# Holding back one unit's loads at the start of a retention and mixer kernel, and moving three small steps of its first stage

## The chip, the cores and the metric

The kernel runs on one core of a Trainium2 chip. The metric is the device time of one execution in microseconds. Five runs of the kernel before gave 327.78 to 331.32 us, median 329.55 us.

The core has a matrix engine (PE, with its weight loads shown apart as PEld), a vector engine (DVE), a scalar engine (ACT), a general engine (POOL, GpSimd) and a synchronising engine (SP). Each works through its own instructions in order. In this kernel SP issues the loads of q, k and v and the DMA transposes; GpSimd issues the loads of the two weights and most stores. All transfers share the core's 16 DMA engines.

## What is computed

Two layers, one behind the other. The first is causal retention with a decay per head, over 8 batches, 8 heads, 576 positions and 64 features:

```python
scores = scale * np.matmul(q, k.transpose(0, 1, 3, 2))
gamma = 1.0 - 2.0 ** (-5.0 - np.arange(H, dtype=np.float32))
rel = pos[:, None] - pos[None, :]
Dmat = np.where(rel >= 0, gamma[:, None, None] ** rel[None, :, :], 0.0)
x = np.matmul(scores * Dmat, v)      # then heads side by side: (8, 576, 512)
```

The second mixes positions through a rank of 32 and then channels through a hidden layer of 2048:

```python
h = x.transpose(0, 2, 1) @ U @ V
u = x + h.transpose(0, 2, 1)
out = u + np.maximum(u @ w_ch1, 0.0) @ w_ch2
```

The decay from position j to position i is a product of a power of gamma at i and one at -j. So the kernel scales keys or values by `vscale` (gamma to the power -j, with the softmax-like scale in it) and outputs by `qscale` (gamma to the power i), and needs only a 0/1 triangle between them.

## The kernel before

Batches go in pairs. A pair has 2 x 576 = 1152 positions, nine chunks of 128; chunk 4 (J) is half of one batch and half of the other. `LO` is its lower half of the partitions (the end of the first batch), `HI` its upper half.

The steady part (from `first_stretch`'s end on) handles a chunk so: `load` brings q, k, v (SP), `cast_chunk` casts them to bf16 on ACT and DVE and scales the values on POOL, `xbar` transposes q and k with a DMA (L289, SP), and `section` does scores, state and outputs on PE. `merge` interleaves these steps with the two large matmuls of the mixer, `y1` (L525) and `y2` (L559), by fixed costs; the order on each engine is then the order of the program.

The first pair is different. Its eight whole chunks are taken as four units of 256 positions, numbered 0 to 3: units 0 and 1 are the first batch, 2 and 3 the second. Positions of a unit lie two to a partition. `load_u` (L615) loads a unit in six tiles, two halves of heads for each of k, q and v. `scale_u` (L643) scales the keys by the decay on POOL, `cast_u` (L636) casts q and v, `T_u` (L652) transposes with PE, `SC_u` and `mask_u` make scores, `RV_u` multiplies them with v, `ST_u` (L766) adds keys times values into a state in PSUM, `Sblk` (L776) copies the state to SBUF, `QS_u` multiplies queries with it, and `XS_u` multiplies the result by `qscale` and writes x. The functions with `_J` do the same for one half of chunk J.

`startup` (L867) writes the order by hand. It first puts all loads on SP: units 0 and 1, chunk J, unit 2, unit 3. On POOL it puts the casts of each unit in turn with pieces of the weight loads between them (`load_w1`, L194; for unit 2 the pieces 4 to 6, 6 to 8 and 8 to 10, for unit 3 the pieces 10 to 12 and 12 to 16), and all of the second weight's loads behind. PE computes the first batch's x, mixes it and gives the transposed result `uT`. `first_stretch` (L990) then works through units 2 and 3 on PE with blocks f = 0 to 15 of `y1` between their steps (`y(n)`: the next n blocks). Blocks 2 and 3 come between unit 2's transposes and its scores, block 4 behind those scores, 5 and 6 behind that; unit 3's transposes follow, then blocks 7 to 12 among unit 3's steps. Block f needs its piece of the first weight. `first_stretch` also puts the loads of the first four chunks of the second pair on SP, behind unit 3's loads.

Of the kernel before, what the change touches and what calls it, by code (L numbers as in the profile page):

```python
# [12 lines left out]
ALU = mybir.AluOpType  # L13
# [21 lines left out]
def kernel(  # L35
# [193 lines left out]
                    in_=dram[b, :, t0:t0 + n, :].rearrange("h s d -> s h d"),  # L229
                )  # L230

    def cast_qk(pr, i, rows=slice(0, P), eng_k=nc.vector, eng_q=nc.scalar):
        c = ch[pr, i]
        if "qk" not in c:
            c["qk"] = qk_pool.tile([P, 2, dm], BF16, tag="qk", name="qk")
        t = c["qk"]
        for j, e in ((1, eng_k), (0, eng_q)):
            o, f = t[rows, j, :], c["f", j][rows].rearrange("p h d -> p (h d)")
            if e is nc.scalar:
                nc.scalar.activation(out=o, in_=f, func=AF.Copy)  # L240
            else:
                e.tensor_copy(out=o, in_=f)
# [369 lines left out]
    def unit_i0(u):  # L612
        return 2 * u + (1 if u >= 2 else 0)

    def load_u(u, which):  # L615
        b = u // 2
        t0 = 2 * P * (u % 2) + HALF * b
        for j in which:
            dram = (q, k, v)[j]
            for hh in range(2):  # L620
                t = stage.tile([P, H, D], FP32, tag="stage", name="stage_t")
                un[u]["f", j, hh] = t
                nc.sync.dma_start(  # L623
                    out=t.rearrange("p (h j) d -> p h (j d)", j=2),
                    in_=dram[b, 4 * hh:4 * hh + 4, t0:t0 + 2 * P, :].rearrange(
                        "h (p j) d -> p h (j d)", j=2),
                )
# [53 lines left out]
    def SC_u(u, hh, pool_, tag):  # L681
        psc = pool_.tile([P, 2, NHP, P], FP32, tag=tag, name="psc")
        kT, qt = un[u]["T", 1], qT(u)
        for hp in range(2):
            for jj in range(2):
                for s in range(2):
                    for hl in range(2):
                        r = slice(hl * HALF, (hl + 1) * HALF)
                        m = slice(s * HALF, (s + 1) * HALF)
                        nc.tensor.matmul(  # L690
                            psc[m, hl, hp * 2 + jj, :], kT[r, jj * NHP + 2 * hh + hp, m],
                            qt[r, 2 * hh + hp, s * P:(s + 1) * P], start=True, stop=True,
                        )
        un[u]["psc", hh] = psc

    def mask_u(u, hh):
        ret = ret_pool.tile([P, H, P], BF16, tag="ret", name="ret")
        nc.vector.tensor_tensor(  # L698
            out=ret.rearrange("p (a j) i -> p a (j i)", j=2),
            in0=un[u]["psc", hh].rearrange("p a b i -> p (a b i)").rearrange(  # L700
                "p (a ji) -> p a ji", a=4),
            in1=triU.rearrange("p j i -> p (j i)")[:, None, :].to_broadcast([P, 4, 2 * P]),
            op=ALU.mult,
        )
        un[u]["ret", hh] = ret
# [60 lines left out]
    def ST_u(u, rows, acc, start, hps=range(4)):  # L766
        for hp in hps:
            for jj in range(2):
                nc.tensor.matmul(
                    acc[:, hp, :], un[u][1][rows, jj, hp * P:(hp + 1) * P],  # L770
                    un[u][2][rows, jj, hp * P:(hp + 1) * P],
                    start=(start and hp == 0 and jj == 0), stop=True,
                    skip_group_check=True,
                )

    def Sblk(acc, slot):  # L776
        for hl in range(2):
            r = slice(hl * HALF, (hl + 1) * HALF)
            nc.scalar.activation(
                out=sblk[r, slot, :, hl * D:(hl + 1) * D],  # L780
                in_=acc[r, :, hl * D:(hl + 1) * D], func=AF.Copy)
# [57 lines left out]

    def XS_J(r):  # L840
        c = ch[0, J]
        nc.vector.tensor_tensor(
            out=st["x", 0][r, J, :].rearrange("p (h d) -> p h d", d=D),
            in0=c["po"][r, :].rearrange("p (h d) -> p h d", d=D),
            in1=qscale[r, J, :, None].to_broadcast([HALF, H, D]), op=ALU.mult,
        )
# [19 lines left out]

    def startup():  # L867
        load_u(0, (1, 0))
        load_v_rows()
        load_u(1, (1, 0))  # L870
        load_u(0, (2,))
        load(0, J, (1, 0), seg=0)
        load_u(1, (2,))
        load(0, J, (2,), seg=0)
        load_u_rows()
        load(0, J, (1, 0, 2), seg=1)
        load_u(2, (1, 0, 2))
        load_u(3, (1, 0, 2))
        nc.gpsimd.memset(st["x", 0][HI, J, :], 0.0)

        warm(10)
        cast_unit(0)
        T_u(0, 1, nc.vector)
        un[0]["off"] = y1_tile(0)[:, 0:4, :].rearrange(
            "p (a x) (y i) -> p a (x y) i", x=2, i=P)
        nc.vector.memset(un[0]["off"][HI], 0.0)
        warm(5)
        nc.scalar.activation(out=V_b, in_=V_f, func=AF.Copy)
        T_u(0, 0, nc.scalar)
        make_v()  # L890
        warm(5)
        SC_u(0, 0, ps_sc, "psc")
        mask_u(0, 0)
        cast_unit(1)
        cast_u(0, 2, 0, nc.gpsimd)
        cast_u(0, 2, 1, nc.gpsimd)
        cast_u(1, 2, 0, nc.gpsimd)
        load_w1(0, 2)
        cast_u(1, 2, 1, nc.gpsimd)
        T_u(1, 1, nc.scalar)  # L900
        SC_u(0, 1, ps_o, "po")
        mask_u(0, 1)
        SC_off(0, ps_sc, "psc")
        warm(3)
        T_u(1, 0)
        SC_off(1, ps_o, "po")
        warm(3)
        SC_u(1, 0, ps_sc, "psc")
        mask_u(1, 0)
        SC_u(1, 1, ps_o, "po")  # L910
        mask_u(1, 1)
        cast_qk(0, J, LO, nc.scalar, nc.scalar)

        acc1 = pss_tile()
        ST_u(0, ALL, acc1, True)
        Sblk(acc1, 1)
        RV_u(0, 0)
        RV_u(0, 1)
        RV_off()
        XS_u(0)  # L920
        T_J(LO)
        acc2 = ps_big.tile([P, NHP, P], FP32, tag="big", name="pss2")
        ST_u(0, ALL, acc2, True)
        prep_v(0, J, LO)
        cast_urows()
        RV_u(1, 0)
        SC_J(LO)
        mask_J(LO)
        for hp in (0, 2):
            ST_u(1, LO, acc1, False, (hp, hp + 1))  # L930
            if hp == 2:
                Sblk(acc1, 2)
            ST_u(1, ALL, acc2, False, (hp, hp + 1))
        Sblk(acc2, 3)
        cast_qk(0, J, HI, nc.gpsimd, nc.gpsimd)
        prep_v(0, J, HI)
        load_w1(2, 4)
        for u in (2, 3):
            for hh in range(2):
                scale_u(u, hh, nc.gpsimd)  # L940
            load_w1(4 if u == 2 else 10, 6 if u == 2 else 12)
            for hh in range(2):
                cast_u(u, 0, hh, nc.gpsimd)
            load_w1(6 if u == 2 else 12, 8 if u == 2 else 16)
            cast_u(u, 2, 0, nc.gpsimd)
            cast_u(u, 2, 1, nc.gpsimd)
            if u == 2:
                load_w1(8, 10)
        for f in range(0, NF, 2):
            load_w2(f)  # L950
        RV_u(1, 1)
        QS_u(1, 0, 1)
        XS_u(1, 0, 1)
        RV_J(LO)
        QS_u(1, 1, 2)
        XS_u(1, 1, 2)
        QS_J(3)
        XS_J(LO)

        xT = [ps_big.tile([P, dm], FP32, tag="big", name="xT") for _ in range(3)]  # L960
        xT.append(ps_sc.tile([P, dm], FP32, tag="psc", name="xT"))

        def to_xT(lo, hi):
            for i in range(lo, hi):
                for cc in range(NCC):
                    nc.tensor.matmul(
                        xT[cc][:, i * P:(i + 1) * P],
                        st["x", 0][:, i, cc * P:(cc + 1) * P], ident,
                        start=(i == 0), stop=True, skip_group_check=True,
                    )  # L970

        to_xT(0, 2)
        MA, _, _, _ = mixer_items(0, 0, split=True)
        MA((ps_o, "po"))
        to_xT(2, J)
        for cc in range(NCC):
            g = slice(cc * R, (cc + 1) * R)
            nc.tensor.matmul(
                xT[cc], st["a", 0][g, :], V4[g, HALF:HALF + 4 * P],
                start=False, stop=True, skip_group_check=True,  # L980
            )
        for cc in range(NCC):
            o = st["uT", 0][:, :, cc, :]
            i_ = xT[cc].rearrange("p (s t) -> p s t", t=P)
            if cc % 2 == 0:
                nc.scalar.activation(out=o, in_=i_, func=AF.Copy)
            else:
                nc.vector.tensor_copy(out=o, in_=i_)
# [129 lines left out]
```

## Time and profile before

| what | us |
|---|---|
| median of five runs | 329.55 |
| the profiled execution | 330.45 |
| its span | 328.7 |
| PE busy | 313.4 |
| DVE busy | 170.3 |
| ACT busy | 143.9 |
| POOL busy | 102.1 |
| PE idle for weight loads (L525) before 80 us | 3.4 |
| unit 3's first load issued by SP | 24.62 |
| its scores' transposes done on PE | 43.24 |
| first chunk of the second pair used by PE | 71.54 |

The span is the time between the first and the last instruction that the profiler recorded; the execution's own time has 1.75 us more around it. A busy time is a sum over an engine's instructions. What a stage is limited by is read from the waits in it: the idle time before an instruction, and what released it.

### The profile page before, as it was taken

The numbers are of one execution on the slowest core, as the hardware profiler recorded it, in microseconds if no ns is written. First come the engines' busy times: TensorE is split into PE (matmuls) and PEld (weight loads), VectorE is DVE, ScalarE is ACT, GpSimd is POOL, SyncE is SP. The second block draws the span as 40 slices with busy tenths as digits, with TensorE's granted clock in tenths as the row PEclk, the third lists the DMA queues.
The fourth block names the chain that finished last, engine by engine and source line by source line (L and its number), as shares of the span: only waits on it lengthen the run. The fifth ranks groups of instructions, "written<-read, shape, count | busy, mean of one in ns | idle before, by whom it ended". The sixth has DMA issues, their size and how long they took to land.

```text
span 328.7 us, 9095 instructions
## 1 busy us (share of the span) xinstructions
PE 313.4 (95%) x3860; PEld 171.6 (52%) x3885; DVE 170.3 (52%) x332; ACT 143.9 (44%) x326; POOL 102.1 (31%) x170
## 2 busy tenths in 40 slices
PE   7998799999999999999999999999999999999996
PEld 3574454665444445456754444456744444467544
DVE  7663256625844477546764377546744475510022
ACT  2837355886002186028820385048810473037400
POOL 7579560342111733223421324142321500110000
PEclk9999799999999999999999999999999999999999
DMA  8999999896992989998999599868997460340012
GB/s 215 231 198 254 224 207 201 189 178 117 205 243 86 242 194 173 211 204 154 201 183 209 130 158 224 206 152 155 208 205 166 124 52 16 92 119 0 2 72 88
DMA packets 152904, 53.30 MB, mean 162 GB/s; under 512 B 132032, under 2 KB 150336, under 8 KB 152864
## 3 DMA queue, kind: packets, MB, share of 16 engines
q1 hardware_dynamic: 144512, 40.40, 66.3%
q0 software_dynamic: 8352, 12.32, 16.0%
q8 instruction: 30, 0.49, 0.7%
q14 instruction: 10, 0.08, 0.1%
HBM read 36.85 MB, written 9.44 MB: 141 GB/s over the span
## 4 chain that ended last, share of the span: by engine, by line
PE 77%; DMA 7%; SPq 5%; ACT 4%; DVE 3%; issue 2%; POOL 1%; DVEq 0%
PE ps_y L525 34%; PE ps_y L559 33%; SPq L623 3%; DMA w_sb<-in_moe_w_ch_dram 2%; PE pp L306 2%; DMA stage_t<-in_v_dram 2%; SPq L227 2%; DVE u L474 2%; ACT y L530 2%; DMA qkT<-qk 1%; PE pp L326 1%; DMA stage_t<-in_q_dram 1%; PE pp L338 1%; PE ps_y L570 1%; PE AB L368 1%
## 5 line engine op out<-in xcount | busy, mean ns | idle before, releaser
L525 PE MATMUL ps_y<-uT,w_sb 128*128 128x256 bf16 (+2 forms) x768 | 133.8, 328 | 5.0 <-DMA w_sb<-in_moe_w_ch_dram 3.4
L530 ACT ACTIVATE y<-ps_y 128x384 bf16<-128x384 f32 (+2 forms) x192 | 89.6, 491 | 99.4 <-PE ps_y L525 98.3
L559 PE MATMUL ps_y<-w_sb,y 128*128 128x512 bf16 x535 | 123.8, 379 | 2.2 <-issue 1.1
L525 PEld LDWEIGHTS <-w_sb 128*128 128x128 bf16 x768 | 72.3, 98 | 53.3 <-issue 4.0
L559 PEld LDWEIGHTS <-y 128*128 128x128 bf16 x560 | 52.5, 98 | 61.2
L282 POOL TENSOR_TENSOR vt<-stage_t,vscale 64x256 bf16<-64x256 f32 (+1 forms) x81 | 50.2, 620 | 71.6 <-DMA stage_t<-in_v_dram 55.8
L548 DVE TENSOR_TENSOR o_sb<-ps_y,u 128x512 f32<-128x512 f32 (+2 forms) x38 | 25.2, 664 | 82.4 <-PE ps_y L559 80.1
L551 POOL DMA_DIRECT2D out_dram<-o_sb x31 | 17.1, 553 | 106.8 <-DVE o_sb L548 100.9
L314 DVE TENSOR_TENSOR ret<-pp,triH 128x512 bf16<-128x512 f32 x27 | 18.7, 692 | 25.4 <-PE pp L338 18.9
L474 DVE TENSOR_TENSOR u<-ph,xt 128x768 bf16<-128x768 f32 (+2 forms) x24 | 21.8, 951 | 5.9 <-PE ph L468 5.9
L447 ACT ACTIVATE a_sb<-pa 128x128 bf16<-128x128 f32 x8 | 2.2, 278 | 45.5 <-PE pa L441 45.5
L354 DVE TENSOR_TENSOR xt<-pp,qscale 128x512 bf16<-128x512 f32 x27 | 18.6, 690 | 4.7 <-PE pp L338 4.2
L273 DVE CAST qk<-stage_t 64x256 bf16<-64x256 f32 x54 | 19.9, 368 | 1.2
L348 DVE COPY q<-qkT 64x256 bf16<-64x256 bf16 x48 | 14.3, 298 | 9.9 <-DMA qkT<-qk 8.9
L393 DVE TENSOR_TENSOR s_sb<-AB,Af 64x256 bf16<-64x256 f32 x42 | 17.7, 421 | 2.1 <-ACT s_sb L388 1.5
L274 ACT ACTIVATE qk<-stage_t 128x512 bf16<-128x512 f32 x27 | 16.8, 622 | 0.1
L698 DVE TENSOR_TENSOR ret<-psc,triU 128x1024 bf16<-128x1024 f32 x8 | 9.6, 1222 | 11.8 <-PE psc L690 11.8
L386 ACT ACTIVATE Af<-AB 128x256 f32<-128x256 f32 x24 | 9.2, 385 | 8.0 <-PE AB L368 7.4
L641 POOL CAST qk<-stage_t 128x512 bf16<-128x512 f32 x16 | 9.7, 616 | 7.9 <-DMA stage_t<-in_v_dram 6.4
L271 ACT ACTIVATE qk<-stage_t 128x256 bf16<-128x256 f32 x27 | 11.1, 410 | 0.0
L306 PEld LDWEIGHTS <-qkT 64*64 64x64 bf16 x432 | 5.6, 107 | 10.0 <-issue 8.7
L191 PE MATMUL pw<-ident 128*128 128x512 bf16 x26 | 8.6, 477 | 1.4 <-POOL ident masks.py:199 1.4
(118 smaller groups left out, 214.6 us busy)
## 6 DMA issues: line engine op xcount, KB each, us to landing
stage_t<-in_k_dram SPq DMA_DIRECT2D x32, 256.0 KB, 4.9
stage_t<-in_q_dram SPq DMA_DIRECT2D x32, 256.0 KB, 5.5
stage_t<-in_v_dram SPq DMA_DIRECT2D x32, 256.0 KB, 5.7
out_dram<-o_sb POOLq DMA_DIRECT2D x31, 256.0 KB, 3.4
w_sb<-in_moe_w_ch_dram POOLq DMA_DIRECT2D x14, 256.0 KB, 8.7
stage_t<-in_k_dram SPq DMA_DIRECT2D x8, 128.0 KB, 3.5
stage_t<-in_q_dram SPq DMA_DIRECT2D x8, 128.0 KB, 3.7
stage_t<-in_v_dram SPq DMA_DIRECT2D x8, 128.0 KB, 3.6
```

The lines of the kernel that those rows point to most:

```text
L273: nc.vector.tensor_copy(out=o[to, hl], in_=f[fr, hl])
L274: nc.scalar.activation(out=c["qk"][:, 0, :], in_=c["f", 0].rearrange("p h d -> p (h d)"), func=AF.Copy)
L282: nc.gpsimd.tensor_tensor(out=o[to, hl], in0=f[fr, hl], in1=w[fr, hl, :, None].to_broadcast([n, NHP, D]), op=ALU.mult)
L314: nc.vector.tensor_tensor(out=ret.rearrange("p a b i -> p a (b i)").rearrange("p a (b i) -> p a b i", i=D), in0=pp[:, :, 0:NHP * D].rearra ...
L354: nc.vector.tensor_tensor(out=st["x", pr][:, i, :].rearrange("p (hp hl d) -> p hl hp d", hl=2, d=D), in0=pp[:, :, NHP * D:2 * NHP * D].rea ...
L393: nc.vector.tensor_tensor(out=S_[half(x), 1, :], in0=Bk[half(1 - x)], in1=Af[half(1 - x), now, :], op=ALU.add)
L474: nc.vector.tensor_tensor(out=st["u", par][:, i0 - base:i0 - base + n, w].rearrange("p s (c d) -> p c s d", c=2), in0=ph[k][:, :, 0:n, :], ...
L525: nc.tensor.matmul(ps[:, 0:n, :], w1_sb[:, cc, f * P:(f + 1) * P], st["uT", par][:, c0:c0 + n, cc, :], start=(cc == 0), stop=(cc == NCC - 1),)
L530: nc.scalar.activation(out=st["y1", par][:, f, c0 * P:(c0 + n) * P], in_=ps[:, 0:n, :].rearrange("p s t -> p (s t)"), func=AF.Relu)
L548: nc.vector.tensor_tensor(out=o_sb[:, 0:n], in0=ps[:, 0:n], in1=st["u", par][:, c, w], op=ALU.add)
L551: (nc.sync if last else nc.gpsimd).dma_start(out=out_flat[r0:r0 + P, w], in_=o_sb[:, 0:n])
L559: nc.tensor.matmul(ps, st["y1", par][:, f, c * P:(c + 1) * P], w2_sb[:, f, :], start=(f == 0), stop=(f == NF - 1),)
```

## The change

Four edits, all in the handling of the first pair.

1. `load_u` gets an argument `gate`. If it is an engine, that engine writes one column of the first tile to be loaded just before the loads. The load has to follow that write, and SP's queue keeps the rest behind it. Unit 3's loads are moved from the head of `startup` into the loop over units 2 and 3: there they stand with POOL as the gate, behind unit 2's query casts and the piece 6 to 8 of the first weight. On SP itself the order of the loads does not change.
2. The lower half of chunk J: the queries are multiplied by `qscale` while they are cast, on DVE, between the two masks of unit 1. Before they were cast on ACT behind both masks. The output step `XS_J(LO)` becomes a plain copy on ACT; before it was DVE's multiplication by `qscale`. 
3. Unit 1's state: the matmuls for the lower half (into the first accumulator) are no longer interleaved by heads with those for the whole unit (into the second); the first eight stay, with their copy, and the other eight with theirs move behind the output of unit 1's first chunk.
4. `RV_J(LO)` moves behind the output of unit 1's second chunk.

```diff
-    def cast_qk(pr, i, rows=slice(0, P), eng_k=nc.vector, eng_q=nc.scalar):
+    def cast_qk(pr, i, rows=slice(0, P), eng_k=nc.vector, eng_q=nc.scalar, decay=False):
...
         for j, e in ((1, eng_k), (0, eng_q)):
+            if j == 0 and decay:
+                n = rows.stop - rows.start
+                e.tensor_tensor(
+                    out=t[rows, 0, :].rearrange("p (h d) -> p h d", d=D), in0=c["f", 0][rows],
+                    in1=qscale[rows, i, :, None].to_broadcast([n, H, D]), op=ALU.mult)
+                continue
...
-    def load_u(u, which):
+    def load_u(u, which, gate=None):
...
                 un[u]["f", j, hh] = t
+                if gate is not None:
+                    gate.memset(t[:, 0:1, 0:1], 0.0)
+                    gate = None
                 nc.sync.dma_start(
...
     def XS_J(r):
         c = ch[0, J]
+        if r == LO:
+
+            nc.scalar.activation(out=st["x", 0][r, J, :], in_=c["po"][r, :], func=AF.Copy)
+            return
...
         load_u(2, (1, 0, 2))
-        load_u(3, (1, 0, 2))
...
         mask_u(1, 0)
+        cast_qk(0, J, LO, nc.scalar, nc.vector, decay=True)
         SC_u(1, 1, ps_o, "po")
         mask_u(1, 1)
-        cast_qk(0, J, LO, nc.scalar, nc.scalar)
...
-        for hp in (0, 2):
-            ST_u(1, LO, acc1, False, (hp, hp + 1))
-            if hp == 2:
-                Sblk(acc1, 2)
-            ST_u(1, ALL, acc2, False, (hp, hp + 1))
-        Sblk(acc2, 3)
+        ST_u(1, LO, acc1, False)
+        Sblk(acc1, 2)
...
             load_w1(6 if u == 2 else 12, 8 if u == 2 else 16)
+            if u == 2:
+                load_u(3, (1, 0, 2), nc.gpsimd)
             cast_u(u, 2, 0, nc.gpsimd)
...
         XS_u(1, 0, 1)
-        RV_J(LO)
+        ST_u(1, ALL, acc2, False)
+        Sblk(acc2, 3)
         QS_u(1, 1, 2)
         XS_u(1, 1, 2)
+        RV_J(LO)
         QS_J(3)
```

## The prediction

> **What bounds the kernel now.** I read the busy rows first, then PE's waits, then the chain of waits in the start, then the stages that the chain named. PE is busy 95% of the span, so at most 15 us of 328.7 are to be had, and only where PE waits:
>
> ```profile
> PE 313.4 (95%) x3860; PEld 171.6 (52%) x3885; DVE 170.3 (52%) x332; ACT 143.9 (44%) x326; POOL 102.1 (31%) x170
> PEclk9999799999999999999999999999999999999999
> ```
>
> PE's waits in the first 80 us name one cause over 1.4 us. The second row, one wait of 1.4 us, is the start itself.
>
> ```profile
> PE ps_y L525 <- DMA w_sb<-in_moe_w_ch_dram: 3.4, 2, 2.7
> PE pw L191 <- POOL ident masks.py:199: 1.4, 1, 1.4
> PE ps_y L525 <- ACT y L530: 0.6, 1, 0.6
> ```
>
> PE waits 0.65 us (30.31) and 2.71 us (35.26) for a piece of the first weight. The chain of waits says how that piece comes to be late (start, length in us): GpSimd finishes the half chunk's values, issues a weight load, scales unit 2's keys and issues the next one, whose transfer then takes 8.10 us.
>
> ```profile
> 23.23 1.04 POOL vt L246
> ...
> 25.10 2.02 POOL qk L645 x2
> 27.12 8.10 DMA w_sb<-in_moe_w_ch_dram
> 35.26 1.04 PE ps_y L525 x4
> ```
>
> Why 8.1? The two DMA queues in 29 to 31 us and, below the dots, in 31 to 33 us (packets' bytes and time as a share of 16 engines):
>
> ```profile
> q1 hardware_dynamic: 1022, 0.51, 89.9%
> q0 software_dynamic: 73, 0.04, 13.2%
> ...
> q0 software_dynamic: 423, 0.21, 77.2%
> q1 hardware_dynamic: 516, 0.26, 53.4%
> ```
>
> q1 carries SP's loads, here unit 3's; q0 the weights. The load issued at 27.12 gets nearly nothing until 31. And the wait has a tail, in rows of one microsecond, where the third number from the end is the granted clock:
>
> ```profile
> 36.30:37.30 1.00, 1.00 (x25) 0.77 (x24) 0.00 (x0) 0.95 (x2) 0.69 (x2) 0.74 1.30 213
> 37.30:38.30 1.00, 1.00 (x11) 0.40 (x4) 0.82 (x1) 0.40 (x2) 0.16 (x1) 0.50 1.30 224
> 39.30:40.30 1.00, 1.00 (x23) 1.00 (x22) 0.00 (x0) 0.58 (x1) 0.00 (x0) 0.55 1.35 194
> ```
>
> After the idle stretch PE runs at half clock for 3.5 us. The missing shares are 0.26+0.50+0.50 (38.30 is alike)+0.45 = 1.7 us. The whole stall is thus worth 3.4+1.7 = 5.1 us, if nothing stands behind it.
>
> Something does. The first transposed chunk of the second pair is used by PE at 71.54. Its chain, from the timeline:
>
> ```profile
> 62.87 3.02 SPq L227 DMA_DIRECT2D stage_t<-in_q_dram  x1
> 66.07 1.54 SPq L289 DMA_TRANSPOSE qkT<-qk  x1
> 70.23 0.46 DVE L348 COPY q<-qkT 64x256 bf16<-64x256 bf16 x2 [5.54 <-DMA qkT<-qk]
> 71.54 0.32 PE L306 MATMUL pp<-qkT 64*64 64x64 bf16 x16
> ```
>
> The transpose starts when SP comes to it, behind eleven chunk loads. SP's issues at 32 to 57 us took 3.35, 6.43, 4.45, 6.25 and 4.31 us each against 0.6 to 0.9 for the same size elsewhere: the queue is full. ACT's casts for it ended at 65.05, so compute did not hold it. It lands at 70.2 and leaves PE 71.54-70.2 = 1.3 us.
>
> **The gate.** Unit 3's six loads leave SP's queue at 24.62 and come behind a memset that stands on GpSimd behind unit 2's query casts and the weight load issued at 29.04 (0.74). So it starts near 29.8, takes 0.10 (the row of a 128x1 memset), and SP issues at 30.0: 5.4 us later. Queued behind the waiting load on SP are the other five, the eleven chunk loads (first at 31.58) and the transpose. GpSimd itself pays 0.1 us for what follows.
>
> *Weights.* The load issued at 27.12 finds q1 nearly empty. Its time: the lightest loaded weight load (17.09) landed in 5.9 us, giving 33.0. [...] No row here is below 5.9, so I take 33.0. [...] The 0.65 before it (landing at 30.2 from 24.22, mostly behind unit 2's own loads) I leave. Gain at this matmul 2.2 us, and without the long gap the 1.7 us of clock: 3.9 us until unit 3's transposes.
>
> *Unit 3.* Its second key half was issued 1.1 us after the first and landed 6.5 us later: now 31.1+6.5 = 37.6 (was 32.3). Then scale 1.05, weight issue 0.81, two query casts 0.62 each: 40.7, four transposes 0.35: 41.05, where before they ended at 43.24. Gain left 2.2 us. If the queues just do the same work in another order, keys come at 35.6 and the gain is the full 3.7. The weight load after the scale moves from 33.66 to 37–38.7; f-block 10 needs it at 47.19 less the gain. With 6.0 to 6.7 us (rows of the loads with no other weight load far ahead of them) it lands at 43 to 45.4, the gain is 1.8 to 3.7; with the 8.7 us it had, 47.4 and nothing is left. I take 6.7 and about 2.5 us of gain at 52 us.
>
> *The transpose.* The bytes ahead of it are the same, so it lands at 70.2 again, and PE arrives at 71.54-2.5 = 69.0. PE is in order, so it waits 1.2 us there. Gain kept: 1.3 us. The next transpose lands at 75.6 for a use at 77.18, slack 1.6, which covers 1.3.
>
> **The half chunk.** ACT loses the 0.63 us query cast (64x512), DVE gets a multiply of that shape between two masks of unit 1: nearest row L842, 0.68 (0.58 as two casts of 0.29 at the other end). ACT gets the output copy, between 0.38 (64x256) and 0.60 (128x512, also from PSUM), DVE loses 0.67. The second mask ends at 18.1 instead of 17.4, before its reader at 18.39. **Unit 1's state:** sixteen state matmuls (1.38 us) split into eight before and eight behind the first chunk's output, where PE waited 0.41 us for DVE; the last state copy on ACT moves behind that, before the half chunk's last product. Up to 0.4 us earlier or 0.7 later, at 22 to 24 us. Both count zero: PE then waits for unit 2's query casts (0.26 us at 29.15), which hang on GpSimd's row of 23.23 and what follows it there, untouched. Without that cover they would be worth -0.4 to +0.7 us.
>
> **Sum.** The profiled execution took 330.45 us (span 328.7 and 1.75 around it); less 1.3 is 329.15. It lies 0.9 above the median of the runs, 329.55; from there 328.25, and I say 328.3.
>
> **Rivals.**
>
> *The transposed chunk does not hold PE* (0.17). If SP's late issues come from queue fullness that the new order eases, the transpose moves forward with PE and all of 2.5 to 3.9 us stays: 325.7 to 327.0. For it: after 57 us the issues are fast again (0.80, 0.80, 0.88). Against: SP reached its transpose only at 66, with ACT a microsecond done.
>
> *The weight wait moves* (0.18). With 8.7 us for the delayed load the gain is gone at f-block 10: 329.5.
>
> *The gate gives the weights nothing* (0.08): 8.1 us again, also 329.5.
>
> *Slower* (0.14). Place: PE before the transposed chunk. Mechanism: with SP's load held until 30.0 the DMA engines have only weights to move between about 28 and 31; 30.0-28.7 (unit 2's last values, issued at 23.5, landed 5.2 us later) = 1.3 us of q1's work is lost, the transpose lands at 71.5, and PE, 2.5 to 3.7 us early, stands still so long that the clock drops. Price 1.7 us as at 36 us, plus 0.1: 331.3. [...] If the half-clock stretch falls together with a late weight load it reaches 333.
>
> *Likeliest, as summed* (0.43): 328.3, or 327.3 to 329.5 with the transpose a microsecond off.
>
> **Range and chances.** 326.3 to 331.4 leaves out the better half of the first rival and the end of the slower one. 1% is 3.3 us, about what a measurement of this kernel can tell from no change. Faster by more has 0.15: two thirds of the first rival (0.11) and 0.04 of the likeliest. Slower by more has 0.10: over half of the slower rival (0.08) and 0.02 of the moved wait. Within 1% are the other 0.75.
>
> **What would show it.** PE's wait for the weight falls from 3.4 to about 1 us, and the clock's dent at 36 to 40 us is gone. Unit 3's loads start at 30.0; its keys are scaled about 4 us later; its last transposes are done 2 to 3.7 us earlier. The weight load behind the scale is issued at 37 to 39. SP's first chunk transpose still starts near 66; a new PE wait for it, 1 to 2.5 us, stands at 68 to 71. DVE's idle time before 70.2 stays. I am wrong if that transpose starts well before 65 (more gain), if PE waits again for weights at 44 to 48, or if the half clock reappears anywhere.

## The result and the profile after

The changed kernel took 327.77 us (median of 44 executions, 325.56 to 330.80), the kernel before 329.19 us beside it (79 executions, 326.36 to 332.81). The ratio is 0.9961, 95% interval 0.9944 to 0.9977: 1.3 us faster, with 1.4 us between the medians. A repeat of both gave 0.9961 again (0.9938 to 0.9983). Ratios are worked out from fast executions alone (within 1.5% of the fastest of their kernel), the medians from all, and the counts and means further down from all but two outliers, of 451.8 us (the kernel before) and 796.2 us (an experiment). The prediction was 328.3 us within 326.3 to 331.4, and "within 1%". The size is right. The way to it is only partly the one that was predicted.

The profiled execution of after took 327.66 us (span 325.9), 2.8 us less than the one of before, which is twice what the medians show. Busy time and clock, from the page of after:

```profile
PE 312.2 (96%) x3860; PEld 171.2 (53%) x3885; DVE 167.6 (51%) x332; ACT 144.3 (44%) x326; POOL 102.0 (31%) x171
PEclk9999999999999999999999999999999999999999
```

The dent of the clock is gone in this execution. PE's waits before 80 us in after (total, times, longest in us):

```profile
PE pst L671 <- POOL qk L651: 1.5, 3, 1.0
...
PE pp L312 <- DMA qkT<-qk: 0.9, 2, 0.6
...
PE ps_y L531 <- DMA w_sb<-in_moe_w_ch_dram: 0.4, 1, 0.4
```

Weights cost PE 0.4 us where they cost 3.4. In their place stand waits for query casts (1.5 us, of which 1.04 us are for unit 3's late queries; L651 is the line of before's L641), and a wait for the DMA transpose. The timeline of after from 26 to 40 us (start, length, engine; at the end the idle time before and what ended it):

```profile
26.56 0.80 POOL L196 DMA_DIRECT2D w_sb<-in_moe_w_ch_dram  x1
...
29.20 0.12 POOL L631 MEMSET stage_t<- 128x1 f32 x1
...
29.34 0.92 SPq L633 DMA_DIRECT2D stage_t<-in_k_dram  x2
...
31.67 1.04 PE L531 MATMUL ps_y<-uT,w_sb 128*128 128x512 bf16 x4
...
34.24 2.07 POOL L655 TENSOR_TENSOR qk<-stage_t,vscaleU 128x512 bf16<-128x512 f32 x2 [3.06 <-DMA stage_t<-in_k_dram]
...
36.26 0.80 POOL L196 DMA_DIRECT2D w_sb<-in_moe_w_ch_dram  x1
...
39.07 0.51 PE L671 MATMUL pst<-ident,qk 128*128 128x128 bf16 x6 [1.04 <-POOL qk L651]
```

The gate is the memset at 29.20, and unit 3's loads follow it at 29.34 (24.62 before). The piece issued at 26.56 lands in 4.6 us (8.1 before), and block 4 starts at 31.67 without a wait (35.26 before). The last transposes of unit 3 have to wait 1.04 us for the cast of the second query half, and are done at 39.58 (43.24 before). What the two DMA queues moved from 29 to 31 us, the stretch shown of before, is now nearly weights alone:

```profile
q0 software_dynamic: 562, 0.28, 111.3%
q1 hardware_dynamic: 35, 0.02, 2.9%
```

The first transposed chunk of the second pair, again from the timeline of after (the lines of before stand in the prediction):

```profile
64.93 2.24 SPq L295 DMA_TRANSPOSE qkT<-qk  x1
...
69.25 0.32 PE L312 MATMUL pp<-qkT 64*64 64x64 bf16 x16 [0.61 <-DMA qkT<-qk]
```

SP comes to it 1.1 us earlier than before, and PE 2.3 us earlier, with a wait of 0.61 us.

### The profile page after: what moved, and what is told of

The parts are those of the page before. It is cut to its first block, busy times and chain, and to the rows that moved or that the text cites. A ratio compares the mean times of both kernels' runs of the same rounds, so it can differ in the third digit from the quotient of the medians.

```text
span 325.9 us, 9085 instructions
## 1 busy us (share of the span) xinstructions
PE 312.2 (96%) x3860; PEld 171.2 (53%) x3885; DVE 167.6 (51%) x332; ACT 144.3 (44%) x326; POOL 102.0 (31%) x171
## 4 chain that ended last, share of the span: by engine, by line
PE 77%; DMA 7%; SPq 5%; ACT 4%; DVE 2%; issue 2%; POOL 2%; DVEq 0%; POOLq 0%
PE ps_y L565 36%; PE ps_y L531 32%; SPq L633 3%; DMA qkT<-qk 3%; DMA stage_t<-in_q_dram 2%; DMA stage_t<-in_k_dram 2%; SPq L227 2%; PE pp L312 2%; DVE u L480 2%; ACT y L536 1%; PE pp L332 1%; PE pp L344 1%; PE ps_y L576 1%; PE AB L374 1%; PE pa L447 1%
## 5 line engine op out<-in xcount | busy, mean ns | idle before, releaser
L279 DVE CAST qk<-stage_t 64x256 bf16<-64x256 f32 x54 | 18.9, 351 | 5.2 <-DMA stage_t<-in_k_dram 4.0
L354 DVE COPY q<-qkT 64x256 bf16<-64x256 bf16 x48 | 12.7, 264 | 9.8 <-DMA qkT<-qk 8.8
L651 POOL CAST qk<-stage_t 128x512 bf16<-128x512 f32 x16 | 9.7, 616 | 5.6 <-DMA stage_t<-in_v_dram 4.1
```

The lines of the kernel that those rows point to most:

```text
L279: nc.vector.tensor_copy(out=o[to, hl], in_=f[fr, hl])
```

## The experiments

They ran in three groups (gate alone to the transposes ahead in the kernel before; filler to filler in the changed kernel; the last three), each group beside its own executions of the kernel before: 329.36, 329.43 and 329.69 us. All ratios are to those.

### Which edit, and does the transpose cap it?

**The gate alone**, in the kernel before (`load_u` gets its argument as in the change):

```diff
         load_u(2, (1, 0, 2))
-        load_u(3, (1, 0, 2))
...
+            if u == 2:
+                load_u(3, (1, 0, 2), nc.gpsimd)
```

> Only the gate, added to the kernel before. Theory G (the gate makes all of the gain, held to about 1.3 us by the transpose that PE meets near 70 us): -1.0 to -1.6 us against before, PE's wait for the weights down from 3.4 to about 0.5 us, a PE wait of 0.3 to 1 us for the first chunk transpose, no half clock. Rival J (the half chunk's and unit 1's steps make the gain, since the start's chain is 0.5 to 1 us shorter in the profile after): -0.5 us or less.

Measured: 327.63 us, ratio 0.9942 (0.9920 to 0.9965). Edit 1 alone makes the whole gain. Its timeline at the first transposed chunk:

```profile
63.96 2.00 SPq L289 DMA_TRANSPOSE qkT<-qk  x1
...
68.23 0.32 PE L306 MATMUL pp<-qkT 64*64 64x64 bf16 x16
```

SP is 2.1 us earlier than in before, PE 3.3 us, and PE does not wait there. The chunk does not keep its time when unit 3's loads, which stand ahead of it, start later.

**The gate undone**: the changed kernel with unit 3's loads back at the head of `startup`.

```diff
         load_u(2, (1, 0, 2))
+        load_u(3, (1, 0, 2))
...
-            if u == 2:
-                load_u(3, (1, 0, 2), nc.gpsimd)
```

> The changed kernel with unit 3's loads back at the head of the queue, all else of the change kept. Theory G: within 0.4 us of before, PE waits for weights 3 us or more, half clock behind it as before. Rival J: -0.8 us or more against before, and GpSimd's chain (the half chunk's values, 23.23 before) ends 0.5 to 1 us earlier.

Measured: 329.27 us, ratio 0.9999 (0.9975 to 1.0023). The other three edits do not show in the time. Its profile has the transposed chunk, with every load in its old place, at:

```profile
64.24 1.78 SPq L295 DMA_TRANSPOSE qkT<-qk  x1
...
68.07 0.46 DVE L354 COPY q<-qkT 64x256 bf16<-64x256 bf16 x2 [4.20 <-DMA qkT<-qk]
```

DVE's copy starts when the transpose has landed: at 68.07, against 70.23 in before.

**The transposes ahead**: in the changed kernel the first two chunk transposes stand on SP ahead of the loads of the fourth and fifth chunk of the second pair.

```diff
-        for g in range(NI, NI + 4):
-            load(*order[g], (1, 0, 2) if g < NI + 3 else (1, 0))
+        for g in range(NI, NI + 3):
+            load(*order[g], (1, 0, 2))
...
-            [(0.04, ready(0)), (0.05, fetch(3, (2,))), (0.06, fetch(4, (1, 0))),
-             (0.12, ready(1)), (0.13, fetch(4, (2,))), (0.20, ready(2)),
+            [(0.04, ready(0)), (0.05, fetch(3)),
+             (0.12, ready(1)), (0.13, fetch(4)), (0.20, ready(2)),
```

> The changed kernel; on SP the first two chunk transposes of the second pair stand ahead of the fourth and fifth chunk's loads instead of behind two of each. Theory G with the cap (the transpose's place in SP's queue takes the rest of the gain): the first transpose starts at 62 to 63.5 instead of 64.9, PE has no wait of its own for it, and the time is 0.5 to 1.5 us below the changed kernel, -1.8 to -2.8 against before. Rival (the gain was all that there was, nothing is capped): equal to the changed kernel within 0.3 us.

Measured: 328.00 us, ratio 0.9966 (0.9944 to 0.9988). Its profile has no wait for the transpose left, and the time is the changed kernel's, not 0.5 to 1.5 us below it. The transpose does not cap the gain.

**The same in the kernel before:**

> The same reordering on SP in the kernel before, where PE comes 1.3 us after the transpose has landed. Cap theory: within 0.3 us of before, since the transpose only gets more slack. Rival (an earlier transpose or later loads are worth something by themselves): the same gain or loss as it gives the changed kernel, 0.5 us or more.

Measured: 328.63 us, ratio 0.9982 (0.9952 to 1.0011), which cannot be told from no change. But its profile held a surprise. It has a half-clock stretch at 31.5 to 35.0 us, and no wait over 1.05 us ahead of it.

### The half clock

The granted clock of the executions falls into steps: 1.000 (0.998 and up); about 0.995, which is one half-clock stretch as in the profile of before (1.7 us of 328.7); and 0.99 or less, which is two or a long one (0.990 in the profile of the gate undone, with 6.8 us at half clock). "Lost" is (1 - clock) x span, the mean over the executions.

| kernel | executions | none | one | more | lost, us |
|---|---|---|---|---|---|
| before | 187 | 45 | 106 | 36 | 1.61 |
| change, with its repeat | 66 | 42 | 23 | 1 | 0.70 |
| gate alone | 22 | 17 | 5 | 0 | 0.51 |
| gate undone | 14 | 2 | 10 | 2 | 1.68 |
| transposes ahead | 18 | 12 | 5 | 1 | 0.73 |
| before, transposes ahead | 14 | 7 | 7 | 0 | 0.82 |
| before, with filler | 22 | 18 | 1 | 3 | 0.62 |
| gate later | 22 | 9 | 11 | 2 | 1.35 |
| gate earlier, with its repeat | 44 | 38 | 4 | 2 | 0.37 |
| change, with filler | 22 | 22 | 0 | 0 | 0.15 |
| a piece ahead | 20 | 17 | 3 | 0 | 0.31 |

A row of 14 is rough: the transposes ahead leave the start of before as it is, and still the row has half of before's loss.

In before the medians of the three columns are 327.63, 329.53 and 331.05 us, in the change 327.34, 328.89 and (one execution) 330.66. Over the executions of one kernel a microsecond of lost clock costs 0.98 us (before) and 1.11 us (change). The means of the two kernels are 329.43 and 327.98 us. Of their difference of 1.46 us, 0.91 is lost clock, and 0.55 (0.31 to 0.79) the rest. The gate alone has that rest too: its executions without half clock are 0.56 us (0.11 to 1.02) below before's in the mean.

That is a correlation. Four kernels put it to the test.

**Filler in before**: eleven matmuls of the identity, whose result nobody reads, ahead of block 4. They keep PE busy in the wait and shorten nothing.

```diff
             mask_u(u, 0)
+            if u == 2:
+                pw = ps_o.tile([P, 4, P], FP32, tag="po", name="pw2")
+                for _ in range(11):
+                    nc.tensor.matmul(
+                        pw, ident, ident[:, None, :].to_broadcast([P, 4, P]), start=True, stop=True)
             y(1)
```

> The kernel before with 11 matmuls on the identity (about 2.4 us, results unused) in the place where PE waits for the weights of block 4; no load is moved. Theory C (what the change takes away is the stretch at half clock, 1.7 to 1.9 us in most executions of before; the waiting itself is regained by neither): mean granted clock 1.000 in most executions, -1.0 to -1.8 us against before, as the change gives. Theory W (the waiting for weights is what counts): the filler takes PE's time as the wait did, 0 to +1 us.

Measured: 328.34 us, ratio 0.9982 (0.9958 to 1.0006). 18 of 22 executions now have no half clock, against 45 of 187. The median falls by 1.1 us, as expected of the clock, though the interval of the ratio does not quite leave out no change. The executions without half clock are 0.5 us slower than before's (328.14 against 327.63), as filler that outlasts the wait would make them: it takes 2.55 us in its profile, and block 4 follows it without a wait. No load was moved here, and yet the transposed chunk comes early in its profile:

```profile
63.05 2.09 SPq L289 DMA_TRANSPOSE qkT<-qk  x1
...
67.40 0.46 DVE L348 COPY q<-qkT 64x256 bf16<-64x256 bf16 x2 [4.00 <-DMA qkT<-qk]
```

**The gate later**, behind unit 2's value casts and the piece 8 to 10:

```diff
-            if u == 2:
-                load_u(3, (1, 0, 2), nc.gpsimd)
...
                 load_w1(8, 10)
+                load_u(3, (1, 0, 2), nc.gpsimd)
```

> The changed kernel with the gate two value casts and one weight piece later on GpSimd (about 31.3 instead of 29.2). Unit 3's keys and queries come about 2 us later, so PE waits about 3 instead of 1 us for unit 3's query casts. Theory C: this wait brings the half clock back, now near 40 us, in most executions: +1 to +2.5 us against the changed kernel, 0 to +1 against before. Theory W: +2 us against the changed kernel from the wait alone, with the clock left at 1.000.

Measured: 329.98 us, ratio 1.0011 (0.9982 to 1.0040). The gain is gone. PE's waits in its profile:

```profile
38.18 0.28 PE L671 MATMUL pst<-ident,qk 128*128 128x128 bf16 x2 [1.31 <-POOL qk L655]
39.19 0.51 PE L671 MATMUL pst<-ident,qk 128*128 128x128 bf16 x6 [0.73 <-POOL qk L655]
40.58 0.28 PE L671 MATMUL pst<-ident,qk 128*128 128x128 bf16 x2 [0.87 <-POOL qk L651]
```

The stall has moved from weights to unit 3's keys and queries, and a half clock follows it at 41.2 to 44.6 us.

**The gate earlier**, behind unit 2's key scaling and the piece 4 to 6:

```diff
             load_w1(4 if u == 2 else 10, 6 if u == 2 else 12)
+            if u == 2:
+                load_u(3, (1, 0, 2), nc.gpsimd)
...
-            if u == 2:
-                load_u(3, (1, 0, 2), nc.gpsimd)
```

> The changed kernel with the gate two query casts and one weight piece earlier (about 27.4). Theory C: between the two kernels; the weights of block 4 still come mostly ahead of unit 3's loads, PE's waits for weights and for the query casts are both under 1.5 us, clock 1.000 in at least half of the executions, -0.7 to -1.8 us against before. Rival (only a gate behind the query casts frees the weights): within 0.4 us of before, with the half clock in most executions.

Measured: 327.18 us, ratio 0.9935 (0.9913 to 0.9958), more than was expected. Waits for unit 3's casts over 0.5 us are gone; weights are late again, but at block 2 and at block 10:

```profile
29.59 1.90 PE L531 MATMUL ps_y<-uT,w_sb 128*128 128x512 bf16 x8 [0.65 <-DMA w_sb<-in_moe_w_ch_dram]
43.70 1.04 PE L531 MATMUL ps_y<-uT,w_sb 128*128 128x512 bf16 x4 [1.54 <-DMA w_sb<-in_moe_w_ch_dram]
```

**Filler in the changed kernel**: five of these matmuls ahead of block 4, five between unit 3's key and query transposes.

> The changed kernel with 5 matmuls on the identity ahead of block 4 and 5 between unit 3's key and query transposes, where PE waits about 1 us for a cast. Theory C: the half clock, left in about a third of the changed kernel's executions, goes from nearly all; -0.3 to -0.8 us against the changed kernel, -1.6 to -2.2 against before. Theory W: 0 to +1 us against the changed kernel, since PE only gets more work.

Measured: 327.69 us, ratio 0.9953 (0.9932 to 0.9974). None of its 22 executions has a half clock. It is no faster than the change all the same, against the expectation: its executions take 327.69 us, and the change's without half clock 327.34. What the clock gives, the filler takes.

### Can the earlier gate be bettered, and is it better than the change?

**A piece ahead**: the earlier gate (the lines are against that kernel), with the piece 10 to 12 issued while GpSimd waits for unit 3's keys.

```diff
-            load_w1(4 if u == 2 else 10, 6 if u == 2 else 12)
             if u == 2:
+                load_w1(4, 6)
                 load_u(3, (1, 0, 2), nc.gpsimd)
...
                 load_w1(8, 10)
+                load_w1(10, 12)
```

> The earlier gate again, with the piece 10 to 12 of the first weight issued right behind the piece 8 to 10, ahead of the scaling of unit 3's keys on GpSimd. Theory (what the kernel loses is idle time of PE, and the half clock that a stretch of PE about half idle brings): the wait of 1.54 us at f-block 10 goes, 0 to 0.3 us is left of it; half clock in under a quarter of the executions; 2.0 to 2.8 us below the kernel before, 0.3 to 1.0 below the earlier gate alone. Rival (the piece now shares the DMA engines with unit 3's loads, and pieces 6 to 8 and 8 to 10 or unit 3's keys come later): a wait of 0.5 us or more at block 6 or 8 or for unit 3's keys, half clock more often, equal to the earlier gate alone or above it.

Measured: 327.59 us, ratio 0.9951 (0.9927 to 0.9976), level with the earlier gate beside it (327.60). The wait at block 10 went, and this one came in its profile, at block 4:

```profile
33.28 1.04 PE L531 MATMUL ps_y<-uT,w_sb 128*128 128x512 bf16 x4 [1.17 <-DMA w_sb<-in_moe_w_ch_dram]
```

So the expected gain did not come and the rival fits: in this profile the order only picked who is late.

**The change again, and the earlier gate again**, unchanged:

> The changed kernel once more, unchanged, beside the earlier gate on the same chip. Theory: 1.1 to 1.7 us below the kernel before; about a third of its executions have the half-clock stretch, against about four fifths of the kernel before, and the executions at full clock of both differ by less than 0.4 us. Rival (the transposed chunk caps the gain, the clock is chance): the same difference at full clock too, 1 us or more.

> The gate behind unit 2's key scaling and the piece 4 to 6, once more and unchanged, beside the change itself. Theory (no wait for unit 3's casts is worth about 0.3 to 0.8 us more than the change): 1.7 to 2.3 us below the kernel before and 0.3 to 0.8 below the change, half clock in under a quarter of the executions. Rival (the difference between the two calls was chance): equal to the change within 0.2 us.

Measured: the change 328.17 us, ratio 0.9961 (0.9938 to 0.9983), 12 of 22 without half clock; the earlier gate 327.60 us, ratio 0.9943 (0.9920 to 0.9966), 20 of 22. Between the two lie 0.57 us of the medians and 0.35 of the means, with an interval of the means from 1.13 faster to 0.46 slower. Over both groups the medians differ by 0.68 us (1.18 faster to 0.09 slower). The earlier gate is probably a little better; it is not shown.

This time the profiled execution of the change has the stretch. Its rows of one microsecond (length, then busy time with instructions of PE, PEld, DVE, ACT and POOL; the third number from the end is the granted clock):

```profile
27.60:28.60 1.00, 0.43 (x6) 0.26 (x6) 0.53 (x1) 0.57 (x2) 1.00 (x2) 1.00 1.20 175
28.60:29.60 1.00, 0.43 (x5) 0.27 (x6) 0.16 (x1) 0.00 (x0) 1.00 (x3) 1.00 0.94 112
29.60:30.60 1.00, 0.45 (x7) 0.28 (x6) 0.00 (x0) 0.60 (x1) 1.00 (x3) 1.00 1.37 172
30.60:31.60 1.00, 1.00 (x5) 0.47 (x6) 0.00 (x0) 0.71 (x1) 1.00 (x3) 0.86 0.88 92
31.60:32.60 1.00, 1.00 (x4) 0.30 (x2) 0.00 (x0) 0.60 (x1) 0.36 (x1) 0.50 1.25 165
```

PE is less than half busy for three microseconds, by waits of 0.87 us at most: for unit 2's query casts and the piece of block 2. Then it runs at half speed.

## Why the prediction was right, and where it was not

**The stall.** 3.4 us of waits and 1.7 of clock were what the one profile of before showed. Over 187 executions the clock part is 1.61 us on average, but it is spread: none in 45, two or a long one in 36.

**The gate.** Predicted SP's issue at 30.0 behind a memset of 0.10 us; 29.34 and 0.12.

**Weights.** Predicted by the row of 5.9 us: a landing at 33.0, and from it a wait of 0.5 us at block 4 in place of 2.71, the gain of 2.2. No run shows that 0.5. The piece landed in 4.6 us with the queues nearly to itself (SP's loads took 2.9% from 29 to 31 us), and the wait it left was none. The next clause, "without the long gap the 1.7 us of clock", was mis-sized: 0.91 us of clock were won. Before does not lose 1.7 us in every execution, and 24 of 66 executions of the change still have a stretch.

**Unit 3.** Predicted were keys landed at 35.6 to 37.6 us and the last transposes done between 39.5 and 41.05. The keys were scaled from 34.24 to 36.31, so the second half had landed when its scaling began, by 35.3; the transposes ended at 39.58: the upper end of the gain of 2.2 to 3.7 us. Some 0.8 us of it came before the gate could act (block 0 starts at 24.57 instead of 25.35). Its price was seen too: PE's waits for unit 3's late queries. The weight piece behind the scaling was issued at 36.26 (37 to 38.7 predicted) and landed 7.8 us later, at 44.04, for a use at 44.09, where PE had waited 0.57 us, by the profile for the state copy. The rival *the weight wait moves* missed by that little; with the earlier gate it came true, with 1.54 us.

**The transpose.** This step failed. It said that the transpose lands at 70.2 again because the bytes ahead are the same, and caps 2.5 us of gain at 1.3. SP came to it at 64.93, not at 66; PE waited 0.61 us, not 1.2, and had 2.3 us of gain behind it. With the gate alone there is no wait at all, and moving the transposes ahead gains nothing. Nor does the transpose need the gate to move: with the loads where before has them it landed by 68.07 (gate undone) and 67.40 (filler in before) instead of 70.2, so the bytes ahead do not fix its time. ACT's cast is not out of it either: with the gate undone it ended at 64.22, and the transpose started at 64.24. At this place the rival *the transposed chunk does not hold PE* was right in its outcome. Why SP's queue comes forward was not tried and stays open. And the chunk can hold PE: in the profile of the earlier gate's repeat, an execution of 331.22 us, PE waits 2.1 us for it.

**The sum.** That it met the median so closely is in part luck: two terms missed in opposite directions. The 1.2 us taken off at the transpose were not lost there. But the gain ahead of it, from an execution of before with the stretch to one of after without it, is not the gain of the mean. For that pair of profiles the sum without a cap was good: 2.5 us expected, 2.3 measured at the chunk, 2.8 at the end. Over all executions it is 1.46 us: 0.91 of clock and 0.55 of the rest, which fits shorter waiting. The waiting that left (2.71 us at block 4) is largely given back at unit 3's casts, the state copy and the transposed chunk: from 12 to 80 us PE is busy 61.70 us in the profile of before and 62.49 us in that of after, 0.79 us less idle. The later and the earlier gate show the trade.

**Half chunk and state.** Counted at zero. With the gate undone they give 329.27 against 329.36 us: no change, known to 0.8 us. They do shorten the start: block 0 begins at 24.0 to 25.1 us in the nine profiles with these edits and at 25.0 to 25.6 us in the four without, by 0.8 us in the mean. What is left of that at the end is too little to be seen.

**The slower rival.** Nothing of it is in the result of the change. It priced one long stand of PE at the chunk: the earlier gate again has a wait of 2.1 us there and the clock stays at 1.00, while the stretch in the change again came behind waits of 0.87 us at most. The line "if the half clock reappears anywhere" came true in a third of the executions (24 of 66); in the one profile of these, the idle time lay at unit 2's transposes and block 2, which the prediction had left as they were.

## What to carry to other kernels

Before a stall is priced from one profile, look at the granted clock of all executions: a half-clock stretch that comes and goes took 1.7 us of clock in four profiles here, and a change may gain by making it rarer rather than by shortening a wait. Add up PE's short waits, and do not look for the longest gap alone: in the change again the half clock followed waits of 0.87 us at most, with PE busy for 1.73 us of 3.41. When transfers are held back in a saturated start, ask who is served late instead, and try the gate at an earlier and a later place: here the later one gave all of the gain back.

## What the runs showed of the hardware

Half-clock stretches lasted 3.4 us in every profile that had one (6.8 us with the gate undone). Not all of them had a long gap ahead: in before there was a wait of 2.71 us, but in the transposes ahead in before, the change again and the gate undone no wait of PE in the 4 us ahead of the stretch was over 1.05, 0.87 and 0.85 us. PE's least busy time in any 3.4 us between 12 and 80 us was, in profiles with a stretch behind it: 0.69 (before), 0.79 (gate later), 1.40 (transposes ahead in before), 1.64 (change again) and 1.74 us (gate undone). Without a stretch: 1.26 (earlier gate again), 1.60 (change with filler), 1.70 (a piece ahead), 1.71 (transposes ahead), 1.86 (gate earlier), 1.91 (gate alone), 2.28 (change) and 2.68 us (filler in before). So the least busy time alone does not decide.

The 3.41 us right ahead of a stretch and the 3.41 us behind, in the change again and then with the gate undone, where the half clock goes on behind the second row (columns as above):

```profile
27.92:31.33 3.41, 1.73 (x15) 0.86 (x13) 0.69 (x1) 1.57 (x2) 3.41 (x8) 1.00 1.07 132
31.33:34.74 3.41, 3.41 (x25) 1.21 (x23) 0.77 (x1) 1.19 (x2) 0.63 (x1) 0.50 1.06 208
...
27.71:31.13 3.41, 1.75 (x14) 0.89 (x14) 0.69 (x1) 1.75 (x3) 3.41 (x6) 1.00 1.19 278
31.13:34.54 3.41, 2.66 (x22) 0.90 (x21) 0.96 (x1) 1.19 (x2) 3.40 (x5) 0.50 1.32 231
```

And the least busy 3.41 us of two profiles that were as idle or more, at full clock all the same: a piece ahead and, below the dots, the earlier gate again.

```profile
26.45:29.86 3.41, 1.71 (x22) 1.09 (x21) 0.69 (x1) 1.89 (x4) 3.41 (x8) 1.00 1.22 166
...
67.52:70.93 3.41, 1.27 (x11) 0.70 (x9) 0.02 (x1) 2.22 (x6) 1.84 (x3) 1.00 1.20 238
```

So in these profiles half clock followed PE's being about half busy (1.73 and 1.75 us of 3.41), with no long wait in it, but not each time (1.71 and 1.27 us). What else decides, and why one kernel has a stretch in some executions only, these rows do not show.
